# Two convs at a time: pairing the convolution steps of a fused dynamic-conv and feed-forward kernel

## The chip, the cores and the metric

The kernel runs on one core of one Trainium2 chip. The core has five engines with a queue each: TensorE (PE; its weight loads are shown as PEld), VectorE (DVE), ScalarE (ACT), GpSimd (POOL) and SyncE (SP). Each works through its own instructions in order and waits on semaphores for the others. The metric is the device time of one execution in microseconds; the median of three runs of the kernel before is 729.72 us (729.19 to 730.9).

## The reference

```
# x (8, 4096, 192), weight_gen (8, 4096, 8 heads, 7 taps), w_in (192, 2048), w_out (2048, 192)
w = softmax(weight_gen over the 7 taps)
x_pad = x with 6 zero rows ahead of each sequence
y[b, s, h, :] = sum over k of w[b, s, h, k] * x_pad[b, s + k, 24 columns of head h]
out = (max(y @ w_in, 0) ** 2) @ w_out        # y as 32768 rows of 192
```

Each token has its own seven weights for each of eight heads; the result goes through a feed-forward layer with squared ReLU.

## The kernel before

The 32768 tokens are cut into sub-blocks of 512 tokens. Blocks 0 and 1 have one sub-block, blocks 2 to 32 have two (`BLOCKS`), so block j, from 2 on, holds sub-blocks 2j - 2 and 2j - 1. Blocks are worked on in an interleaved order that the program writes out by hand (`tc.manual_schedule()`): each engine's instructions stand in the order in which the program issues them. There is one such order for each block, a string of steps (`plans[j]`), in which

- `u` is a unit (`st_unit`, line 571): six matmuls of 512 columns, with 64-row weights in two row halves, make 128 hidden features of the block's 1024 tokens in a two-bank PSUM tile `h`. ScalarE applies ReLU into `t1` (line 595), and VectorE squares two units at a time into `g` (line 599). 16 units make a block: u0 to u15 below.
- `M` is half a quarter of the second matrix product of the block before (`st_mm2`, line 611): 32 matmuls of 192 columns (line 630) that read 8 of the 16 chunks of `g`. Two M make a quarter: the first reads chunks 0 to 7, the second 8 to 15. They add up in the two PSUM banks `o0` and `o1`, of which there is one each. After the second M `o_sum` has ScalarE copy `o0` (line 644) and VectorE add `o1` (line 646), and only then can the next quarter's first M write there. M0 to M7 below; the sums follow M1, M3, M5 and M7, and after M3 and M7 SyncE stores the result (line 651).
- `C` is the conv of the next block (`st_conv_spread`, line 481, from block 8 on): 80 matmuls with 32-column weights taken from `x`, moving the band tiles `bd`. They fill two PSUM tiles `yp` of two banks, of which ScalarE copies the first to SBUF and VectorE the second (line 512). Then SyncE moves a few rows inside `y` (line 516, four DMAs).
- `B` is the band work of one sub-block (`st_bands`, line 658): VectorE multiplies the softmax rows `wr` with a mask into a band tile `bd` (line 406), in one instruction, or in two where a batch begins or ends. The conv needs both band tiles of its block.
- `L`, `E`, `S` are load, exponentials (ScalarE, line 244) and the rest of the softmax on VectorE (lines 251, 258, 266) of one piece of a batch's tokens. A batch from number 3 on has pieces of 8, 10, 10 and 10 rows for each partition. After its last piece the weights are stored to DRAM (line 280), and SyncE loads rows of them (`wr_load`, lines 317 to 327), which the bands read.

`h`, `yp` share three two-bank tiles of PSUM that go round (tag `h`), `o0` and `o1` are the other two banks. In the steady state a block's order is

```
steady_spread = "MuMuuu" * 2 + "MuCMuuu" + "MuMuuu"
```

that is M0 u0 M1 u1 u2 u3, M2 u4 M3 u5 u6 u7, M4 u8 C M5 u9 u10 u11, M6 u12 M7 u13 u14 u15. Steps B, E, S and L are put ahead of a unit by `at(j, u, kind, ...)`, line 769: the bands of block j + 1 ahead of units 1 and 5 of block j, the four softmax pieces of a batch whose first block is f ahead of unit 9 of blocks f - 5 to f - 2 (`TIMES`, line 775, gives other places to the early batches). `x_load` (line 329, on GpSimd's queue) follows the conv, and `load_rows` (line 826) asks at the start of block j for the rows of block j + 2.

Of the kernel before, what the change touches and what calls it, by code (L numbers as in the profile page):

```python
# [9 lines left out]
def kernel(  # L10
# [35 lines left out]
    G = D // H  # L46
    SPREAD = H - 2
    FIRST_SPREAD = 8
    HP = H // 2

    P = 128
# [344 lines left out]
    def st_band(j, tiles):  # L396


        if j not in bd_t:
            bd_t[j] = p_bd.tile([P, H * NT * STEP], f16, name="bd")  # L400
        i = tiles[0]
        lo = STEP * i
        shift = 0 if i == 0 and j % NBB == 0 else lo - tile_start(j, i)
        n = min(STEP, P - shift)
        shape = (P, HP * len(tiles), n // SL, 2 * SL)
        nc.vector.tensor_tensor(  # L406
            out=bd_t[j][:, H * lo : H * (lo + len(tiles) * n)].rearrange(
                "p (g m c) -> p g m c", g=shape[1], c=2 * SL
            ),
            in0=wr_t[j][:, i : tiles[-1] + 1]  # L410
            .rearrange("p t g c -> p (t g) c")
            .unsqueeze(2)
            .broadcast_to(shape),
            in1=mask[:, shift : shift + n]
            .rearrange("p (m c) e -> p m (c e)", c=SL)
            .unsqueeze(1)
            .broadcast_to(shape),
            op=AluOp.mult,
        )
# [58 lines left out]
        else:  # L478
            nc.scalar.copy(out=y[:, 0:2], in_=yp)

    def st_conv_spread(j):

        s0, n = BLOCKS[j]
        y = p_y.tile([P, NK + 1, TB], f16, name="y")
        y_t[j] = y
        for ks in ((NK, NK - 1), (0, 1)):
            yp = ps_h.tile([P, 2, TB], f32, name="yp", tag="h")
            k0 = min(ks)
            for k in ks:
                for i in range(NT):  # L490
                    a, b = bounds[i], bounds[i + 1]
                    for half in (0, 1):
                        s = s0 + half
                        hi = a + (STEP if tile_start(s, i) == starts[i] else b - a)
                        bd = bd_t[s][:, H * a : H * hi].rearrange(
                            "p (g c e) -> p g e c", g=HP, e=2
                        )
                        for e in (0, 1):
                            head = 2 * k + e
                            p0 = RT * half + 32 * e  # L500
                            c0 = min(G * head, D - 32)
                            nc.tensor.matmul(  # L502
                                out=yp[p0 : p0 + 32, k - k0, a:b],
                                lhsT=x_t[s][:, i, c0 : c0 + 32],
                                rhs=bd[:, head // 2, e, 0 : b - a],
                                start=True,
                                stop=True,
                                skip_group_check=True,
                                tile_position=(0, p0),
                            )  # L510
            copy = nc.vector.tensor_copy if k0 == 0 else nc.scalar.copy
            copy(out=y[:, k0 : k0 + 2], in_=yp)  # L512
        for p0 in range(0, P, 32):
            head = SPREAD + p0 // 32 % 2
            r0 = p0 + G * head - min(G * head, D - 32)
            nc.sync.dma_start(out=y[p0 + G : p0 + 32, 0:NK], in_=y[r0 : r0 + G, NK])

    def st_conv(j):

        if j >= FIRST_SPREAD:  # L520
            return st_conv_spread(j)
# [144 lines left out]
    with nc.allow_low_precision("fp16 matmul pipeline"), tc.manual_schedule():  # L666
# [80 lines left out]
        for q in range(4):  # L747
# [7 lines left out]

        steady = "MuMuuu" * 3 + "MuuuMCu"
        steady_spread = "MuMuuu" * 2 + "MuCMuuu" + "MuMuuu"
        plans = {
# [10 lines left out]
        def at(j, u, kind, *args):  # L769
# [26 lines left out]
        for n, s in enumerate(parts[4:], 4):  # L796
            b, f = s.b, s.fb
            k = n - min(m for m, p in enumerate(parts) if p.b == b)
            times = TIMES.get((b, k)) or (
                (f - 5, 9), (f - 4, 9), (f - 3, 9), (f - 2, 9)  # L800
            )
            assert len(times) == len(s.pieces)
            for j, u in times:
                at(*exp_time(j, u), "E", n)
                at(j, u, "S", n)
            at(times[0][0] - 1, 0, "L", n)
        for j in range(len(plans), NBLK - 1):
            a = BLOCKS[j + 1][0]
            small = [p for p in parts if p.fb <= j + 1][-1].r == FIRST
            us = {4: (7, 9), 6: (7, 9)}.get(j, (5, 9) if small else (1, 5))  # L810
            if j + 1 >= FIRST_SPREAD:
                us = (1, 5)
            for n, u in enumerate(us):
                at(j, u, "B", a + n)
        for j in range(len(plans), NBLK):
            plan, u = [], 0
            for step in steady_spread if j + 1 >= FIRST_SPREAD else steady:
# [56 lines left out]

        mm2 = quarters()
        for j in range(NBLK):
            if j + 2 < NBLK:
                load_rows(j + 2)
            if j == 1:
                for q in range(WQ):  # L880
                    cross_w_in(q)
            u = 0
            for step in plans[j].split():
                kind, n = step[0], int(step[1:] or 0)
                if kind == "u":
                    st_unit(j, u)
                    u += 1
                elif kind == "M":
                    next(mm2)
                elif kind == "C" and j + 1 < NBLK:  # L890
                    st_conv(j + 1)
                    if j == 0:
                        x_load(3)
                    elif j + 2 < NBLK:
                        for k in range(BLOCKS[j + 2][0], sum(BLOCKS[j + 2])):
                            x_load(k)
                    if j == 5:
                        load_w_spread()
                    elif j == 6:
                        cross_w_spread()  # L900
                elif kind == "E":
                    parts[n].exp(*next(parts[n].exps))
                elif kind == "S":
                    soft(parts[n])
                elif kind == "B":
                    st_bands(n)
                elif kind == "L":
                    parts[n].load(nc.sync)
# [47 lines left out]
```

## Time and profile before

The profiled execution has a span of 728.43 us (first to last instruction); the runs, timed around the whole execution, have a median of 729.72 us. The granted TensorE clock is 1.000.

| engine | busy us | share of the span | instructions |
|---|---|---|---|
| PE | 722.0 | 99% | 14078 |
| PEld | 530.1 | 73% | 14078 |
| DVE | 625.8 | 86% | 839 |
| ACT | 612.0 | 84% | 731 |
| POOL | 98.5 | 14% | 146 |

| work | line | engine | count | busy us | mean ns of one |
|---|---|---|---|---|---|
| second product (M) | 630 | PE | 8032 | 380.1 | 243 |
| units, from block 8 on | 581 | PE | 2400 | 291.7 | 376 |
| convs, from block 8 on | 502 | PE | 2000 | 28.4 | 210 |
| ReLU | 595 | ACT | 512 | 496.6 | 1027 |
| square | 599 | DVE | 287 | 307.4 | 1105 |
| bands | 406 | DVE | 90 | 149.5 | 1685 |
| add of o1 | 646 | DVE | 123 | 68.4 | 556 |

How to read it: matmuls are pipelined, so the mean of one is a latency and not its share of the time; what a step costs is read from the distance between starts. [...]

### The profile page before, as it was taken

The page shows a single profiled execution, that of the slowest core. Times are in us where ns is not written, and L with a number is a line of the kernel's source. Part 1 is how long each engine was busy: PE and PEld are TensorE (multiplying, and loading weights), DVE is VectorE, ACT ScalarE, POOL GpSimd, SP SyncE. Part 2 cuts the span into 40 slices and gives each one's busy share as a digit, 9 for nine tenths or more (in the row PEclk, how much of TensorE's full clock was granted, in tenths as well). Part 3 has the DMA queues.
Part 4 walks back from the last instruction along what each step waited for, and adds up shares of the span by engine and source line. Part 5 has one row for each costly group of instructions (what it writes and reads, how often), then busy time and mean ns, then how long its engine had stood idle before and what let it go on. Part 6 is the DMA issues. An engine that isn't in the chain of part 4 may idle for free.

```text
span 728.4 us, 31046 instructions
## 1 busy us (share of the span) xinstructions
PE 722.0 (99%) x14078; PEld 530.1 (73%) x14078; DVE 625.8 (86%) x839; ACT 612.0 (84%) x731; POOL 98.5 (14%) x146
## 2 busy tenths in 40 slices
PE   8999999999999999999999999999999999999998
PEld 5668877777777777777777777777777777777777
DVE  7999997998898998888988888988888988778753
ACT  6998888888888888888888888888888888888883
POOL 7231223411001100011001010010000110001000
PEclk9999999999999999999999999999999999999999
DMA  9664465676245443356432554343544325444112
GB/s 193 128 113 106 82 125 89 128 142 138 78 71 133 99 84 68 75 116 125 83 62 58 135 104 88 66 74 110 114 78 87 57 53 117 67 87 77 30 46 67
DMA packets 126272, 68.30 MB, mean 94 GB/s; under 512 B 85353, under 2 KB 122556, under 8 KB 125628
## 3 DMA queue, kind: packets, MB, share of 16 engines
q0 software_dynamic: 46192, 19.43, 22.9%
q1 hardware_dynamic: 79804, 46.79, 22.5%
q8 instruction: 110, 1.80, 1.1%
q14 instruction: 22, 0.18, 0.1%
q10 hardware_dynamic: 144, 0.10, 0.0%
HBM read 50.18 MB, written 28.70 MB: 108 GB/s over the span
## 4 chain that ended last, share of the span: by engine, by line
PE 98%; DMA 1%; SPq 0%; ACT 0%; issue 0%; ACTq 0%
PE o L630 47%; PE h L581 44%; PE yp L502 4%; PE h L566 2%; PE yp L536 1%; DMA w_st<-in_moe_w_in_dram 1%; SPq L219 0%; PE yp L466 0%; ACT w_i L740 0%; SPq L135 0%; SPq L133 0%; ACT y L476 0%; SPq L327 0%; SPq L317 0%; ACT o_sb L644 0%
## 5 line engine op out<-in xcount | busy, mean ns | idle before, releaser
L595 ACT ACTIVATE t<-h 128x1024 f16<-128x1024 f32 x512 | 496.6, 1027 | 60.1 <-PE h L581 58.4
L630 PEld LDWEIGHTS <-g 64*128 64x128 f16 (+1 forms) x8032 | 344.3, 94 | 55.2 <-issue 2.3
L630 PE MATMUL o<-w_o,g 64*128 64x192 f16 (+1 forms) x8032 | 380.1, 243 | 0.1
L599 DVE TENSOR_TENSOR g<-t 128x2048 f16<-128x2048 f16 (+1 forms) x287 | 307.4, 1105 | 28.7 <-ACT t L595 28.3
L581 PE MATMUL h<-y,w_p 64*128 64x512 f16 x2400 | 291.7, 376 | 0.0
L581 PEld LDWEIGHTS <-w_p 64*128 64x128 f16 x2400 | 113.9, 94 | 94.8
L406 DVE TENSOR_TENSOR bd<-wr,mask 128x4160 f16<-128x4160 f16 (+4 forms) x90 | 149.5, 1685 | 1.2 <-ACT wr L391 1.2
L646 DVE TENSOR_TENSOR o_sb<-o,o_sb 128x384 f32<-128x384 f32 x123 | 68.4, 556 | 61.4 <-ACT o_sb L644 60.3
L327 POOL DMA_DIRECT2D xt<-in_x_dram x63 | 52.6, 838 | 415.4 <-PE yp L502 362.5
L644 ACT COPY o_sb<-o 128x384 f32<-128x384 f32 x129 | 61.6, 477 | 45.7 <-PE o L630 44.4
L581 PE MATMUL h<-y,w_i 64*128 64x512 f16 x576 | 70.5, 376 | 0.0
L581 PEld LDWEIGHTS <-w_i 64*128 64x128 f16 x576 | 30.5, 94 | 21.7 <-issue 1.2
L502 PEld LDWEIGHTS <-xt 128*32 128x32 f16 x2000 | 24.6, 95 | 10.6 <-issue 10.6
L266 DVE TENSOR_TENSOR v_big<-ex,rcp 128x112 f16<-128x112 f32 (+5 forms) x180 | 29.9, 237 | 2.1 <-DMA vd<-v_big 1.1
L512 DVE CAST y<-yp 128x1024 f16<-128x1024 f32 x25 | 30.4, 1218 | 0.0
L502 PE MATMUL yp<-bd,xt 128*32 128x104 f16 (+1 forms) x2000 | 28.4, 210 | 0.0
L244 ACT ACTIVATE ex<-wg 128x560 f32<-128x560 f32 (+5 forms) x40 | 26.3, 659 | 1.2 <-DMA wg<-in_weight_gen_dram 1.2
L251 DVE TENSOR_REDUCE ssum<-ex 128x80 f32<-128x560 f32 (+5 forms) x40 | 25.6, 639 | 1.3 <-ACT ex L244 1.3
L512 ACT CAST y<-yp 128x1024 f16<-128x1024 f32 x25 | 25.2, 1007 | 0.0
L258 DVE RECIPROCAL rcp<-ssum 128x64 f32<-128x64 f32 (+4 forms) x39 | 23.0, 589 | 1.4
L317 POOL DMA_DIRECT2D xt<-in_x_dram x7 | 3.9, 555 | 120.4 <-PE yp L502 109.4
L361 POOL DMA_DIRECT2D wr<-v_first x24 | 13.0, 559 | 24.0 <-DVE v_first L266 23.8
(42 smaller groups left out, 111.9 us busy)
## 6 DMA issues: line engine op xcount, KB each, us to landing
out_dram<-o_sb SPq DMA_DIRECT2D x63, 384.0 KB
xt<-in_x_dram POOLq DMA_DIRECT2D x42, 240.0 KB, 4.9
wg<-in_weight_gen_dram SPq DMA_DIRECT2D x4, 1064.0 KB
xt<-in_x_dram POOLq DMA_DIRECT2D x21, 192.0 KB, 5.0
wr<-vd SPq DMA_DIRECT2D x38, 80.0 KB
vd<-v_big SPq DMA_DIRECT2D x5, 512.0 KB
y<-y SPq DMA_DIRECT2D x100, 24.0 KB
wg<-in_weight_gen_dram SPq DMA_DIRECT2D x3, 616.0 KB
```

The costliest lines, as they stand in the source:

```text
L244: nc.scalar.activation(out=self.ex[:, lo:hi].rearrange("p r g k e -> p (r g) k e"), in_=self.wg[:, lo:hi].rearrange("p r (g e) k -> p (r g ...
L266: eng.tensor_tensor(out=bass.AP(tensor=v.tensor, offset=v.offset + lo * H * SL + lo % SL * 2 + g * SL * 2, ap=[list(v.ap[0]), [H * SL + 2, ...
L327: eng.dma_start(out=dst[:, first:last], in_=ap)
L406: nc.vector.tensor_tensor(out=bd_t[j][:, H * lo : H * (lo + len(tiles) * n)].rearrange("p (g m c) -> p g m c", g=shape[1], c=2 * SL), in0= ...
L502: nc.tensor.matmul(out=yp[p0 : p0 + 32, k - k0, a:b], lhsT=x_t[s][:, i, c0 : c0 + 32], rhs=bd[:, head // 2, e, 0 : b - a], start=True, sto ...
L512: copy(out=y[:, k0 : k0 + 2], in_=yp)
L581: nc.tensor.matmul(out=h[:, half], lhsT=w_in_chunk(w, u, slot, half), rhs=y_t[j][r0 : r0 + RT, k], start=(slot == 0), stop=(slot == NK - 1 ...
L595: nc.scalar.activation(out=t1[:, e], in_=h, func=ActF.Relu)
L599: nc.vector.tensor_tensor(out=g[:, a : e + 1], in0=t1[:, a : e + 1], in1=t1[:, a : e + 1], op=AluOp.mult)
L630: nc.tensor.matmul(out=oo[:, cc * Dm : (cc + 1) * Dm], lhsT=g[r0 : r0 + n, cc * P : (cc + 1) * P], rhs=w_o[r0 : r0 + n, fc, :], start=(fc ...
L644: nc.scalar.copy(out=o_sb, in_=o[0][:, c])
L646: nc.vector.tensor_tensor(out=o_sb, in0=o[1][:, c], in1=o_sb, op=AluOp.add)
```

## The change

From block 14 on every second block (14, 16 ... 30) has a step `D` in place of `C`: it runs the convs of the next two blocks, one right after the other, and the blocks between have no conv. In the order of such a block, D stands behind M5, where C stood ahead of it:

```
steady_pair = "MuMuuu" * 2 + "MuMDuuu" + "MuMuuu"
```

Four PSUM tiles are filled by a pair. Three are `yp` tiles of the ring; the fourth, the last of the second conv, is put into `o0` and `o1`, one bank each, and VectorE copies it in two instructions of 512 columns. Around this:

- bands: those of block j + 2 (not j + 1) are made in block j, ahead of units 1 and 5; of block 15 ahead of unit 13 of block 13 and unit 0 of block 14, of block 16 ahead of units 2 and 6 of block 14. Every fourth band tile from block 15 on is put into the memory of `w_i`, the weights of the units before block 8.
- rows: from block 12 on, those of block j + 3 are asked for (block 12 asks for 14 and 15).
- softmax: the pieces of a batch come one block sooner, in blocks f - 6 to f - 3; for batch 4 (f = 17) ahead of units 1 and 9 of block 12 and unit 9 of blocks 13 and 14.
- x: loaded for two blocks after each D, and for blocks 15 and 16 after the conv in block 13.
- buffers: `p_x` four (before two), `p_wr` six (four), `p_y` three (two).

```diff
-    p_x = ctx.enter_context(tc.tile_pool(name="p_x", bufs=2))
-    p_wr = ctx.enter_context(tc.tile_pool(name="p_wr", bufs=4))
+    p_x = ctx.enter_context(tc.tile_pool(name="p_x", bufs=4))
+    p_wr = ctx.enter_context(tc.tile_pool(name="p_wr", bufs=6))
...
-    p_y = ctx.enter_context(tc.tile_pool(name="p_y", bufs=2))
+    p_y = ctx.enter_context(tc.tile_pool(name="p_y", bufs=3))
...
+        first = BLOCKS[FIRST_PAIR + 1][0]
+        if j not in bd_t and j >= first and (j - first) % 4 == 3:
+            bd_t[j] = w_i.rearrange("p q e c -> p (q e c)")[:, 0 : H * NT * STEP]
...
+    def st_conv_spread(blocks):
+
+        for j in blocks:
+            y = p_y.tile([P, NK + 1, TB], f16, name="y")
+            y_t[j] = y
+            for ks in ((NK, NK - 1), (0, 1)):
+                k0 = min(ks)
+                copy = nc.vector.tensor_copy if k0 == 0 else nc.scalar.copy
+                if j != blocks[0] and k0 == 0:
+                    outs = [ps_o.tile([P, TB], f32, name=f"yo{k}", tag=f"o{k}") for k in ks]
+                    spread_slots(j, ks, outs)
+                    for k, o in zip(ks, outs):
+                        copy(out=y[:, k], in_=o)
+                else:
+                    yp = ps_h.tile([P, 2, TB], f32, name="yp", tag="h")
+                    spread_slots(j, ks, [yp[:, k - k0] for k in ks])
+                    copy(out=y[:, k0 : k0 + 2], in_=yp)
+            spread_rows(y)
...
         steady_spread = "MuMuuu" * 2 + "MuCMuuu" + "MuMuuu"
+        steady_pair = "MuMuuu" * 2 + "MuMDuuu" + "MuMuuu"
+        steady_plain = "MuMuuu" * 4
...
+            (4, 0): ((12, 1), (12, 9), (13, 9), (14, 9)),
...
-                (f - 5, 9), (f - 4, 9), (f - 3, 9), (f - 2, 9)
+                (f - 6, 9), (f - 5, 9), (f - 4, 9), (f - 3, 9)
...
+        a = BLOCKS[FIRST_PAIR + 1][0]
+        at(FIRST_PAIR - 1, 13, "B", a)
+        at(FIRST_PAIR, 0, "B", a + 1)
+        for j in range(FIRST_PAIR, NBLK - 2):
+            a = BLOCKS[j + 2][0]
+            for n, u in enumerate((2, 6) if j == FIRST_PAIR else (1, 5)):
+                at(j, u, "B", a + n)
...
-            if j + 2 < NBLK:
+            if j + 2 < NBLK and j <= FIRST_PAIR - 2:
                 load_rows(j + 2)
+            if j + 3 < NBLK and j >= FIRST_PAIR - 2:
+                load_rows(j + 3)
...
+                elif kind == "D":
+                    if j + 2 < NBLK:
+                        st_conv_spread([j + 1, j + 2])
+                    if j + 4 < NBLK:
+                        for k in range(BLOCKS[j + 3][0], sum(BLOCKS[j + 4])):
+                            x_load(k)
```

`FIRST_PAIR` is 14. `spread_slots(j, ks, outs)` holds the conv's loop of matmuls as it was, for the slots `ks` into the given PSUM tiles, and `spread_rows(y)` the four moves of rows.

More of the change, by code (lines that the diff above doesn't have):

```diff
@@ L48 @@
     FIRST_SPREAD = 8
+    FIRST_PAIR = 14
     HP = H // 2
@@ L479, in st_conv_first @@
             nc.scalar.copy(out=y[:, 0:2], in_=yp)
[L481 to L496, printed above, removed]
-                        )
[L498 to L512, printed above, removed]
@@ new lines, in spread_slots @@
+    def spread_slots(j, ks, outs):
+        s0 = BLOCKS[j][0]
+        for k, out in zip(ks, outs):
+            for i in range(NT):
+                a, b = bounds[i], bounds[i + 1]
+                for half in (0, 1):
+                    s = s0 + half
+                    hi = a + (STEP if tile_start(s, i) == starts[i] else b - a)
+                    bd = bd_t[s][:, H * a : H * hi].rearrange(
+                        "p (g c e) -> p g e c", g=HP, e=2
+                    )
+                    for e in (0, 1):
+                        head = 2 * k + e
+                        p0 = RT * half + 32 * e
+                        c0 = min(G * head, D - 32)
+                        nc.tensor.matmul(
+                            out=out[p0 : p0 + 32, a:b],
+                            lhsT=x_t[s][:, i, c0 : c0 + 32],
+                            rhs=bd[:, head // 2, e, 0 : b - a],
+                            start=True,
+                            stop=True,
+                            skip_group_check=True,
+                            tile_position=(0, p0),
+                        )
@@ L513, in st_conv_spread, with spread_rows @@
+    def spread_rows(y):
         for p0 in range(0, P, 32):
@@ L516, in st_conv_spread @@
             nc.sync.dma_start(out=y[p0 + G : p0 + 32, 0:NK], in_=y[r0 : r0 + G, NK])
+    def st_conv_spread(blocks):
[15 more added lines that the diff above has]
+            spread_rows(y)
     def st_conv(j):
         if j >= FIRST_SPREAD:
-            return st_conv_spread(j)
+            return st_conv_spread([j])
         if j < NFIRST:
@@ L812 @@
                 us = (1, 5)
+            if j >= FIRST_PAIR:
+                break
             for n, u in enumerate(us):
+                at(j, u, "B", a + n)
[5 more added lines that the diff above has]
+            for n, u in enumerate((2, 6) if j == FIRST_PAIR else (1, 5)):
                 at(j, u, "B", a + n)
@@ L816 @@
             plan, u = [], 0
-            for step in steady_spread if j + 1 >= FIRST_SPREAD else steady:
+            form = steady_spread if j + 1 >= FIRST_SPREAD else steady
+            if j >= FIRST_PAIR:
+                form = steady_plain if (j - FIRST_PAIR) % 2 else steady_pair
+            for step in form:
                 if step == "u":
@@ L894 @@
                     elif j + 2 < NBLK:
-                        for k in range(BLOCKS[j + 2][0], sum(BLOCKS[j + 2])):
+                        last = j + 3 if j + 1 == FIRST_PAIR else j + 2
+                        for k in range(BLOCKS[j + 2][0], sum(BLOCKS[last])):
                             x_load(k)
```

## The prediction

> **What bounds the kernel now.** I read first the chain of work that ended last, then the groups by line, then the timelines of TensorE, VectorE and ScalarE block by block, and last SyncE's queue. The chain, by engine:
>
> ```profile
> PE 98%; DMA 1%; SPq 0%; ACT 0%; issue 0%; ACTq 0%
> ```
>
> From 97 us on TensorE's steps repeat to within 0.03 us and none waits for another engine. So time is won only by taking TensorE's steps away, and a wait put in front of TensorE is lost for good. Two groups by line (count | busy us, mean ns of one | idle before):
>
> ```profile
> L512 DVE CAST y<-yp 128x1024 f16<-128x1024 f32 x25 | 30.4, 1218 | 0.0
> ...
> L477 DVE CAST y<-yp 128x512 f16<-128x512 f32 x1 | 0.7, 692 | 0.5 <-PE yp L466 0.5
> ```
>
> One block in the timeline (start us, duration); its first M starts at 406.34, the next block's at 428.41, 22.07 later. TensorE about its conv, then VectorE:
>
> ```profile
> 412.89 0.81 PE L581 MATMUL h<-y,w_p 64*128 64x512 f16 x6
> 413.53 1.49 PE L630 MATMUL o<-w_o,g 64*128 64x192 f16 x32
> 414.85 2.11 PE L581 MATMUL h<-y,w_p 64*128 64x512 f16 x18
> 416.80 1.48 PE L630 MATMUL o<-w_o,g 64*128 64x192 f16 x32
> 418.12 0.81 PE L581 MATMUL h<-y,w_p 64*128 64x512 f16 x6
> 418.86 1.11 PE L502 MATMUL yp<-bd,xt 128*32 128x104 f16 x80
> 419.90 1.49 PE L630 MATMUL o<-w_o,g 64*128 64x192 f16 x32
> ```
>
> ```profile
> 410.33 0.56 DVE L646 TENSOR_TENSOR o_sb<-o,o_sb 128x384 f32<-128x384 f32 x1 [1.50 <-ACT o_sb L644]
> 410.81 2.31 DVE L406 TENSOR_TENSOR bd<-wr,mask 128x4160 f16<-128x4160 f16 x1
> 413.04 2.35 DVE L599 TENSOR_TENSOR g<-t 128x2048 f16<-128x2048 f16 x2
> 415.56 0.56 DVE L646 TENSOR_TENSOR o_sb<-o,o_sb 128x384 f32<-128x384 f32 x1 [0.17 <-ACT o_sb L644]
> 416.04 2.35 DVE L406 TENSOR_TENSOR bd<-wr,mask 128x3328 f16<-128x3328 f16 x2
> 418.30 2.35 DVE L599 TENSOR_TENSOR g<-t 128x2048 f16<-128x2048 f16 x2
> 420.57 1.22 DVE L512 CAST y<-yp 128x1024 f16<-128x1024 f32 x1
> 421.94 0.56 DVE L646 TENSOR_TENSOR o_sb<-o,o_sb 128x384 f32<-128x384 f32 x1
> 422.42 0.73 DVE L251 TENSOR_REDUCE ssum<-ex 128x80 f32<-128x560 f32 x1
> 423.18 0.65 DVE L258 RECIPROCAL rcp<-ssum 128x80 f32<-128x80 f32 x1
> 423.87 1.22 DVE L266 TENSOR_TENSOR v_big<-ex,rcp 128x56 f16<-128x56 f32 x8
> 425.00 2.35 DVE L599 TENSOR_TENSOR g<-t 128x2048 f16<-128x2048 f16 x2
> 427.28 0.55 DVE L646 TENSOR_TENSOR o_sb<-o,o_sb 128x384 f32<-128x384 f32 x1
> ```
>
> Read here: a unit ahead of an M takes 0.64 us (412.89 to 413.53), the same unit ahead of a conv 0.74 (418.12 to 418.86). And VectorE's add of line 646 must come before the next quarter's M: that of 415.56 ends 0.7 us ahead of the M at 416.80. VectorE's long idle time, 1.50 us, lies before M1's add, not after it.
>
> **Removed: two switches for each pair.** In the single matmul records the last unit matmul to the first conv matmul is 0.306 us, to the first M matmul 0.212; the last conv matmul to the first M matmul is 0.137, where four conv matmuls take 0.049 inside a conv (0.929 / 19). So each change between the 64-row and the 32-column form costs about 0.09. A pair of convs back to back has two changes and not four. By transitions: before, two blocks hold 2 x (0.306 + 0.137) and 14 unit-to-M, 16 M-to-unit; after, one M-to-conv (0.172, from the four of the older conv, line 536), one conv-to-unit (0.136), one join (0.049), 16 x 0.212, 15 x 0.079 (M-to-unit). The difference is 0.886 - 0.357 - 0.424 + 0.079 = 0.18. With nine pairs (in blocks 14, 16 ... 30): 1.7 us won. Bounds: 0.17 to 0.23 for a pair, 1.5 to 2.1.
>
> [...]
>
> **Put in place of it: waits of the pair.** Block clock, zero at its first M; M0..M7 and u0..u15 as they come. M5 starts at 12.42 (unit u8 at 11.78 plus 0.65), the pair at 12.42 + 1.24 + 0.17 = 13.83, its second conv at 14.77, its last matmul at 15.70, u9 at 15.84, M6 at 17.78, M7 at 19.75, the next block at 23.01. A matmul that waits for VectorE or ScalarE starts 0.05 after that one's end (11.06 to 11.12 us). ScalarE's copy of an o starts 1.52 after its M, the add of line 646 0.51 later and takes 0.56; a conv tile can be read some 0.23 after its last matmul's start.
> - Fourth tile of the pair, in o0 and o1, from 15.24: M5's add starts at 14.45 (VectorE's g ends at 14.23, as above) and ends at 15.01. Room 0.2.
> - u9 needs the first tile, which ScalarE copies 14.55 to 15.56; room 0.2. u10 (16.49) needs the second, VectorE 14.99 to 16.21; room 0.2. u11 (17.14) needs the third, ScalarE to 16.5.
> - M6 (17.78) needs o1 back. The copy of 1024 columns (1.218) becomes two of 512 (0.692 each by line 477): starts at 16.13 and 16.74, end 17.43. Room 0.3. (At most, if each half took 1.218, o1 would come 0.7 late, 6 us over nine; the row of its own shape decides.)
> - Then a softmax piece of ten rows (422.42 to 425.00: 2.59), two g (1.14 each from start to start) and M7's add, 22.21 to 22.77; the next M0 at 23.01. Room 0.2.
> So nothing waits in these pairs, narrowly; cover gone, each 0.1 us costs up to 0.9 over nine. Bounds: 0 and 0.2 a pair, 1.8 in all; I take 0.
>
> The split copy costs VectorE 2 x 0.692 - 1.218 = 0.166 a pair, 1.5 over nine, inside the 0.3 of room ahead of M6. [...]
>
> **Moved: softmax pieces, and here it costs.** Batch 4's first piece goes to block 12, unit 1. In VectorE's order it stands behind M1's add, ahead of the first band. That add starts at 3.99 (410.33 - 406.34), then: 0.48 to the next, eight rows 1.99 (356.15 to 358.14 in the trace), the band 2.27 (in two pieces, 416.04 to 418.30), two g 2.27. M3's add starts at 11.00, ends at 11.55, and M4, due at 10.46, goes on at 11.60. **Lost: 1.1 us.** Without the piece the add was ready at 9.22. Bounds 0.9 to 1.3 by these rows' spread. Later in that block I find no wait: M5's add ends 0.25 before M6.
>
> **Moved: four bands around the start of block 14.** Beyond block 13's own two they stand at (13, unit 13), (14, 0), (14, 2) and (14, 6). In block 13, after M7's add at 20.94: band 21.41 to 23.64 (2.23), g of u12 and u13 to 24.78, the two single g of 0.61 and 0.68 to 26.07. Block 14's M1 (22.07 + 1.97 = 24.04) reads that last g as its eighth chunk at 25.13; it goes on at 26.2. **Lost 1.05.** The band of (14, 0) then runs 26.0 to 28.23, M1's add 28.23 to 28.79, and M2, now due at 28.4, starts at 28.84. **Lost 0.45.** After that, M4 has 0.25 of room, and the pair finds M5's add done 0.3 ahead of need. Bounds: 0 if a band could hide in idle time (there are 1.5 us of it in a block, all before M1's add, and 2.23 + 2.23 don't fit), 2.2 if M2 waits the whole second band; I take 1.5 by the row sum.
>
> **Other moves, costed at nothing.**
> - SyncE: a pair issues eight y moves (0.72 each, 5.75 together) ahead of the softmax store, not four: from 16.3 to 22.0. The store of batch b goes out at 22.1, not 18.8. It takes 3.4 to land (425.12 to 428.48), the row loads, the second issued 0.4 after the first, 1.6 and 2.1 (landed 430.07 and 430.96): at 27.1 and 27.9. The bands that read them come at 27.47 and 28.0, where 2.4 us were to spare. Past that, VectorE has 0.2 before M3's add and M4 0.6 after it. If the landing is 1.8 later, 1 us is lost in each of the four blocks 14, 18, 22, 26.
> - x on GpSimd, with four buffers: its wait for the conv (362.5 us on line 327) becomes shorter, and the loads (4.9 us to land) have a block or more before use. Rows of the block three ahead: six buffers, more lead. The fourth band in w_i, which nothing reads after block 7: same instruction. ScalarE's exponentials move a block; its conv copies stay 1.0 us each, two in a row after M5, counted above.
>
> **Sum.** -1.7 + 1.1 + 1.05 + 0.45 = +0.9 us on a profiled span of 728.43: 729.3. The median of the runs is 729.72, 1.3 above that span (start and end around it); I keep this 1.3: **730.6 us**.
>
> **Rivals.**
> 1. *Faster: the waits of blocks 12 to 14 are not there.* For it: VectorE sits idle 1.5 us before M1's add, and 86% busy is an average. Against: the order is fixed, and the idle time lies ahead of that add. With no such wait 729.72 - 1.7 = 728.0. 13%.
> 2. *Slower: VectorE's queue behind each pair.* One mechanism, in each of blocks 14 to 30: after the pair come three copies in a row and, up to block 26, the softmax piece and two g ahead of M7's add. It decides once VectorE is 0.2 us later than in my sum. For it: four rooms of 0.2 to 0.3 in a row. Against: the row of line 477, and that VectorE reaches 14.23 in all blocks I compared. If it is 0.5 late, 0.3 x 9 = 2.7 on top: 733.3. 25%.
> 3. *The pair saves nothing:* the change of form is hidden by the reorder of weight loads (their engine idles 10.6 us before line 502, 0.42 each). Against: 0.306 and 0.212 are starts of matmuls, on the engine that bounds. It would give 729.72 + 2.6 = 732.3. 4%.
>
> **How the numbers follow.** My forecast has 58%; its own range is 729.6 to 732.0 (saving 1.5 to 2.1, blocks 12 to 14 2.0 to 3.2, pairs 0 to 0.6). Runs can't tell changes under 0.2% (1.46 us) apart: 728.26 to 731.18 counts as the same. The forecast puts 0.46 in it and 0.12 above. Rival 2 (0.25) and 3 (0.04) add to slower: 0.41. Rival 1 has its 0.13 about the limit at 728.26; I give 0.12 to faster, 0.01 to the same, which has 0.47. The range 728.2 to 733.2 leaves out half of rivals 1 and 2.
>
> **What would show it.** In the changed profile: nine runs of 160 conv matmuls, 0.17 after an M and 0.14 before a unit; in block 12 an M4 (some 10.5 us after the block's M0) that starts about 1.1 late behind VectorE's line of the add; in block 14 an M1 that stretches from 1.24 to some 2.3 us, and an M2 0.45 late; elsewhere no M or unit waiting. The forecast is wrong if TensorE waits in every pair for o1 or a conv copy, if bands wait for rows from DRAM in blocks 15, 19, 23, 27, or if M4 of block 12 is on time.

## The result: slower by 1.5%

| kernel | median of the runs, us | runs | span of the profiled execution, us | granted clock |
|---|---|---|---|---|
| before | 729.82 (729.19 to 730.9) | 4 | 728.4 | 1.000 |
| changed | 740.7 (740.05 to 741.25) | 4 | 739.4 | 1.000 |

The ratio is 1.0148, with a 95% interval of 1.0134 to 1.0163. The forecast was 730.6, with a range up to 733.2: the change costs some 11 us where 0.9 was expected.

### The profile page after: what moved, and what is told of

Same layout as the page of the kernel before. It is cut to its first block, busy times and chain, and to the rows that moved or that the text cites. A ratio compares the mean times of both kernels' runs of the same rounds, so it can differ in the third digit from the quotient of the medians.

```text
span 739.4 us, 31005 instructions
## 1 busy us (share of the span) xinstructions
PE 723.9 (98%) x14078; PEld 553.5 (75%) x14078; DVE 627.4 (85%) x848; ACT 613.6 (83%) x731; POOL 98.3 (13%) x146
## 4 chain that ended last, share of the span: by engine, by line
PE 51%; DVE 3%; DMA 3%; issue 1%; SPq 0%; ACT 0%
PE o L649 26%; PE h L600 23%; PE yp L501 2%; DMA vd<-v_big 1%; DVE g L618 1%; DMA y<-y 1%; DVE bd L410 1%; DMA wr<-vd 1%; PE yo L501 0%; DVE v_big L267 0%; DVE y L534 0%; DVE y L530 0%; SPq L516 0%; DVE o_sb L665 0%; DVE rcp L259 0%
## 5 line engine op out<-in xcount | busy, mean ns | idle before, releaser
L649 PEld LDWEIGHTS <-g 64*128 64x128 f16 (+1 forms) x8032 | 363.9, 94 | 51.7 <-issue 8.2
L649 PE MATMUL o<-w_o,g 64*128 64x192 f16 (+1 forms) x8032 | 397.3, 243 | 4.7 <-DVE o_sb L665 4.2
L600 PE MATMUL h<-y,w_p 64*128 64x512 f16 x2400 | 308.3, 376 | 2.2 <-issue 1.9
L600 PEld LDWEIGHTS <-w_p 64*128 64x128 f16 x2400 | 135.0, 94 | 90.5 <-issue 2.7
L410 DVE TENSOR_TENSOR bd<-wr,mask 128x4160 f16<-128x4160 f16 (+4 forms) x76 | 128.9, 1715 | 6.9 <-DMA wr<-vd 6.1
L501 PE MATMUL yp<-bd,xt 128*32 128x104 f16 (+1 forms) x1460 | 22.5, 209 | 0.0
L410 DVE TENSOR_TENSOR w_i<-wr,mask 128x3328 f16<-128x3328 f16 (+2 forms) x14 | 21.0, 1531 | 0.0
```

The source lines that it names most:

```text
L410: nc.vector.tensor_tensor(out=bd_t[j][:, H * lo : H * (lo + len(tiles) * n)].rearrange("p (g m c) -> p g m c", g=shape[1], c=2 * SL), in0= ...
L501: nc.tensor.matmul(out=out[p0 : p0 + 32, a:b], lhsT=x_t[s][:, i, c0 : c0 + 32], rhs=bd[:, head // 2, e, 0 : b - a], start=True, stop=True, ...
L600: nc.tensor.matmul(out=h[:, half], lhsT=w_in_chunk(w, u, slot, half), rhs=y_t[j][r0 : r0 + RT, k], start=(slot == 0), stop=(slot == NK - 1 ...
L649: nc.tensor.matmul(out=oo[:, cc * Dm : (cc + 1) * Dm], lhsT=g[r0 : r0 + n, cc * P : (cc + 1) * P], rhs=w_o[r0 : r0 + n, fc, :], start=(fc ...
```

## The profile after

The chain of work that ended last, by engine, in the changed kernel. It reaches back only to 302.5 us, so its shares add up to some 59% of the span and can't be set beside the 98% for TensorE before, where the chain goes back to the start:

```profile
PE 51%; DVE 3%; DMA 3%; issue 1%; SPq 0%; ACT 0%
```

TensorE is still busy for 723.9 us (722.0 before), so it was given no more work. It waits. Its waits in the changed kernel (line, what was waited for: us in total, times, longest):

```profile
PE o L649 <- DVE o_sb L665: 4.2, 5, 1.5
PE yo L501 <- issue: 2.3, 3, 1.1
PE h L600 <- issue: 1.9, 2, 1.1
```

None of the three rows is there before. "issue" means that nothing in the profile ended the wait. To place each wait, I compared the distance from every unit's first matmul to the next one's in the two traces, from block 2 to block 32. The differences add up to 11.3 us (the first of these units is 0.35 earlier, which leaves the 10.9 between the spans):

| where | us | what ends the wait |
|---|---|---|
| nine pairs, by themselves | -2.0 | a block with an unhindered pair is 0.95 longer, the one after it 1.15 to 1.20 shorter |
| block 12, M4 and the conv behind it | +1.3 | the add of line 665 |
| block 14, M1 and M2 | +1.45 | the last g (0.93), the add (0.52) |
| block 6, the M that starts at 134.01 | +1.7 | the add, behind a band that waited for its rows |
| in or behind the pairs of blocks 14, 16, 22, 24, 30 | +5.25 | "issue": 0.7, 1.1, 1.3, 1.3, 0.9 |
| M4 of blocks 19 and 27 | +1.9 | the add, behind bands that waited for rows |
| first unit of blocks 19 and 21 | +0.7 | the y moves |
| M5 ahead of the pairs of blocks 18, 22, 26, 30 | +0.8 | not found: 1.62 us to the pair's first matmul, 1.41 to 1.52 in the other five |
| all else | +0.15 | differences under 0.08 each |

The first three rows are the forecast's own terms (-1.7, +1.1, +1.5). In TensorE's timeline of the changed kernel (start us, duration) the waits of blocks 12 and 14 look like this; an M that waits is split into its first matmul and the rest:

```profile
263.49 0.24 PE L649 MATMUL o<-w_o,g 64*128 64x192 f16 x1
264.66 1.48 PE L649 MATMUL o<-w_o,g 64*128 64x192 f16 x31 [0.93 <-DVE o_sb L665]
...
300.48 1.82 PE L649 MATMUL o<-w_o,g 64*128 64x192 f16 x28
302.56 0.34 PE L649 MATMUL o<-w_o,g 64*128 64x192 f16 x4 [0.26 <-DVE g L618]
...
304.68 0.24 PE L649 MATMUL o<-w_o,g 64*128 64x192 f16 x1
305.26 1.48 PE L649 MATMUL o<-w_o,g 64*128 64x192 f16 x31 [0.34 <-DVE o_sb L665]
```

M1 of block 14 does not stop in one place: its first 28 matmuls stretch over 1.82 us, where all 32 take 1.48 elsewhere.

The other rows, some 10 us, are missing from the forecast's sum. All but the last two of them have three sources.

**Block 6.** VectorE's timeline, changed and then before:

```profile
131.78 2.33 DVE L410 TENSOR_TENSOR bd<-wr,mask 128x4160 f16<-128x4160 f16 x1 [1.81 <-DMA wr<-vd]
```

```profile
130.25 2.32 DVE L406 TENSOR_TENSOR bd<-wr,mask 128x4160 f16<-128x4160 f16 x1
```

The same band starts 1.5 us later because its rows do, though they were asked for 3.6 us sooner (121.93 and not 125.52 on SyncE's queue). What is new beside them is GpSimd's copy of `w_p` (weights of the units), two transfers of 384 KB:

```profile
121.79 1.31 POOL L171 DMA_DIRECT2D w_p<-w_p  x2
```

With two x buffers GpSimd's next x loads waited for a conv (at 95 and 118 us before) and held everything behind them on its queue. With four they don't: the loads of `w_p` begin at 104.3 and not at 120.2, and this copy comes at 121.8 and not at 144.7, while SyncE reads the rows. TensorE's M then waits for the add behind the band:

```profile
135.76 1.48 PE L649 MATMUL o<-w_o,g 64*128 64x192 f16 x31 [1.51 <-DVE o_sb L665]
```

The copy is named by its time alone: the x loads asked for just ahead of it (119.58 to 121.82, and 142.48 before) came sooner too, and no run tells the two apart.

**Rows and y moves from block 14 on.** SyncE's queue at the pair of block 18, changed and then a block with the same store before: y moves, the softmax store, the first row load, which waits for the store to land:

```profile
406.30 5.72 SPq L516 DMA_DIRECT2D y<-y  x8
412.13 0.39 SPq L281 DMA_DIRECT2D vd<-v_big  x1
417.60 0.34 SPq L318 DMA_DIRECT2D wr<-vd  x1
```

```profile
421.86 2.83 SPq L516 DMA_DIRECT2D y<-y  x4
425.12 0.34 SPq L280 DMA_DIRECT2D vd<-v_big  x1
428.50 0.35 SPq L317 DMA_DIRECT2D wr<-vd  x1
```

From store to row load it takes 5.5 us and not 3.4. The DMA queue with the x loads (packets, MB, share of 16 engines) from 405 to 420 us, and the same from 418 to 432 us before, shows twice the traffic:

```profile
q0 software_dynamic: 2640, 0.98, 58.2%
```

```profile
q0 software_dynamic: 1328, 0.49, 31.8%
```

The x loads of two blocks start as soon as the pair has read the old ones (405.23), beside the store. The bands that read the late rows then hold up the add, and the add M4 of block 19:

```profile
419.27 0.59 DVE L410 TENSOR_TENSOR bd<-wr,mask 128x832 f16<-128x832 f16 x1 [1.27 <-DMA wr<-vd]
420.09 1.89 DVE L410 TENSOR_TENSOR bd<-wr,mask 128x3328 f16<-128x3328 f16 x1 [0.23 <-DMA wr<-vd]
...
424.17 0.55 DVE L665 TENSOR_TENSOR o_sb<-o,o_sb 128x384 f32<-128x384 f32 x1
...
424.77 1.42 PE L649 MATMUL o<-w_o,g 64*128 64x192 f16 x30 [0.63 <-DVE o_sb L665]
```

**Waits that nothing ends.** TensorE at the pair of block 16 in the changed kernel:

```profile
358.65 1.18 PE L501 MATMUL yp<-bd,xt 128*32 128x104 f16 x82
...
360.67 0.82 PE L600 MATMUL h<-y,w_p 64*128 64x512 f16 x5
362.29 1.68 PE L600 MATMUL h<-y,w_p 64*128 64x512 f16 x13 [0.80 <-issue]
```

The pair itself runs through, 320 instructions (160 weight loads, 160 matmuls) in 1.87 us. Then unit 9 stops after five of its six matmuls, in the middle of a group whose data is there. The profile's list of DMA queues has one whose kind is named for what could be missing:

```profile
q8 instruction: 110, 1.80, 1.0%
```

110 packets of 16384 bytes. Over TensorE's 28156 loads and matmuls that is 64.0 bytes for each, so 256 to a packet. That the queue is TensorE's is an estimate from this agreement; no view says it. Set beside the five waits (times from the trace's packets and matmuls):

```
pair in block   packet from, to   TensorE stops, goes on   goes on after the packet's end
14              313.70  314.64    315.43  316.13           1.49
16              359.68  360.93    361.11  362.29           1.36
22              494.00  494.93    495.12  496.39           1.46
24              539.96  540.89    540.82  542.32           1.43
30              673.22  674.54    674.94  675.85           1.31
```

And counted in program order from the first one of the trace (TensorE's few semaphore instructions included), all five stops are at instruction 194 or 195 of a group of 256, a weight load and its matmul. By the same count the pairs begin at instruction 182, 190 and 198 of their group (blocks 14, 22, 30), 120 and 128 (16, 24), 58 and 66 (18, 26), 252 and 4 (20, 28); only the first two kinds stop.

## The experiments

Each expectation names its own theories; a letter does not stand for the same one in all of them. Of the edits the main lines are shown: e1 is set against the kernel before, e2 to e7 against the changed kernel, e9 and e8 against e7, e10 against e8, e11 against e10. "Before" was run again beside each set: 730.22 (e1 to e4), 729.55 (e5 to e8), 729.74 us (e9 to e11).

**e1_px4: the kernel before, with four x buffers alone.**

```diff
-    p_x = ctx.enter_context(tc.tile_pool(name="p_x", bufs=2))
+    p_x = ctx.enter_context(tc.tile_pool(name="p_x", bufs=4))
```

> The kernel before with four x buffers in place of two, nothing else. In the profile of the changed kernel block 6, long before the first pair, has a wait of 1.7 us: VectorE stood 1.81 us ahead of a band until rows that SyncE had asked for at 121.93 us landed at 131.76, while GpSimd's 768 KB of w_p to w_p copies ran from 121.8 to 131.6. In the kernel before, GpSimd sent these copies later, because its x loads waited for a conv. Theory A (the buffers let GpSimd run ahead, and its copies collide with the row loads): about 731.5, +1.7 us over before, with the wait in block 6. Rival B (the wait comes from another part of the change, such as p_wr or p_y): as before, 729.8, and no wait in block 6.

731.22 us, ratio 1.0014 (1.0004 to 1.0024). In its trace block 6 is 2.24 longer, by a wait of the same M, nothing else moves by more than 0.2 and the start is 0.64 shorter. The buffers alone make the wait of block 6.

**e2_shift: 128 more TensorE instructions ahead of everything.** The warm-up's matmuls are narrower and more.

```diff
-        WARM = 156
+        WARM = 64
...
-        spin(46)
+        spin(110)
```

> The changed kernel with 110 warm-up matmuls of 64 columns in place of 46 of 156: 128 TensorE instructions more (a load and a matmul each) ahead of everything, so that all later ones stand 128 further along the 256-instruction (16 KB) pieces in which the queue of instruction loads brings them; nothing else moves. In the changed kernel five TensorE waits that no engine ends (0.7 to 1.3 us, after the pairs of blocks 14, 16, 22, 24, 30; 5.2 us in all) stop at places 194 or 195 of 256. Theory A (the pair uses up instructions faster than they are loaded): the waits leave 14, 16, 22, 24, 30 and appear in blocks 18, 20, 26, 28; four of them, total 739 to 741. Rival B (contention with the x loads or another transfer after the pair): the same five blocks wait, 740.7.

741.25 us, 1.0148 (1.0115 to 1.0182). The waits without a releaser left blocks 14, 16, 22, 24 and 30 and came up in 18, 20, 26 and 28 (matmul gaps of 0.82, 1.52, 0.60, 1.95 us):

```profile
PE yo L501 <- issue: 2.8, 3, 1.7
PE h L600 <- issue: 1.1, 1, 1.1
```

These are exactly the pairs that now begin where the stopping ones did, at 186 and 194 (blocks 18, 26) and 124 and 132 (20, 28), and they stop at instruction 194 or 195 again. Only the place in the stream was changed for these pairs, and the waits went with it, as theory A has it. The total stayed, because where a pair no longer stopped, rows or y moves were late (0.37 to 1.3 us in blocks 17, 19, 23, 25).

**e3_half: a conv of half as many instructions.** From block 15 on one matmul of 64 weight columns stands for the two of 32; the second head of each pair of heads is not computed.

```diff
+                    w = 64 if j > FIRST_PAIR else 32
-                    for e in (0, 1):
+                    for e in (0,) if w == 64 else (0, 1):
...
-                            out=out[p0 : p0 + 32, a:b],
-                            lhsT=x_t[s][:, i, c0 : c0 + 32],
+                            out=out[p0 : p0 + w, a:b],
+                            lhsT=x_t[s][:, i, c0 : c0 + w],
```

> The changed kernel whose convs from block 15 on have one matmul with 64 weight columns where there were two with 32 (the second head of a pair of heads gets the first one's band, so its part of the conv is not computed). The moving columns and so the time of a conv stay, but a pair issues 160 TensorE instructions, not 320. Theory A (instruction supply): no wait without a releasing engine after any pair; 5.2 us less, 735 to 736. Rival B (contention after the pair): the five waits stay, 740 to 741.

No pair is followed by a wait without a releaser: the theory of the instruction supply holds again. The time is 740.25 (1.0102 to 1.0176), a miss: M4 of blocks 23 and 27, on time or 1.0 late in the changed kernel, is 2.1 and 2.3 late here, of blocks 15 and 19 0.7. TensorE came sooner to bands whose rows came no sooner.

**e4_xlate: the x loads moved in the program.** They follow unit 9 of the next block in the order in which the program issues them.

```diff
-        steady_plain = "MuMuuu" * 4
+        steady_plain = "MuMuuu" * 2 + "MuMuXuu" + "MuMuuu"
...
-                    if j + 4 < NBLK:
-                        for k in range(BLOCKS[j + 3][0], sum(BLOCKS[j + 4])):
+                elif kind == "X":
+                    if j + 3 < NBLK:
+                        for k in range(BLOCKS[j + 2][0], sum(BLOCKS[j + 3])):
                             x_load(k)
```

> The changed kernel with the x loads of a pair sent a block later (behind unit 9 of the odd block, still 20 us ahead of use) and not right after the pair. In the changed kernel the softmax store after the pairs of blocks 18 and 26 took 5.4 and 5.1 us to land where 3.4 were measured before, so that bands and with them M4 of blocks 19 and 27 came 0.95 late, and u0 of blocks 19 and 21 waited 0.3 and 0.4 for y rows. Theory A (the four x loads crowd out the store and the y moves): these waits vanish, 2.5 us less, 738; the waits without a releaser stay, since they are not contention. Rival B (the eight y moves ahead of the store on SyncE's queue are all of it): they stay, 740.7. Rival C (the x loads also hold up the instruction loads): the five waits without a releaser vanish too, 733.

741.03 us. But the edit did nothing: GpSimd has nothing else to do there and asks for x when the buffers come free, at 315.69 us as at 315.27, wherever the program writes it. So this tells no theory apart. It is a second execution of the same schedule, and shows how much rows vary: M4 of block 19 was 0.2 late (0.94 in the changed kernel), of 27 1.7 (0.97), of 15 0.6 (0).

**e5_xgate: x held back for good.** A copy of one column on GpSimd, which needs g of unit 9 of the odd block, stands ahead of the x loads at step X.

```diff
+                elif kind == "X":
+                    if j + 3 < NBLK:
+                        nc.gpsimd.tensor_copy(out=gate, in_=g_t[(j, 9)][:, 0, 0:1])
+                        for k in range(BLOCKS[j + 2][0], sum(BLOCKS[j + 3])):
+                            x_load(k)
```

> The x loads of a pair held back on GpSimd until g of unit 9 of the odd block is there (a one-column copy of that g into gate stands ahead of them), so that they no longer run beside the pair's row moves and the softmax store. Theory D (two blocks of x, 0.98 MB, fill the DMA engines while the 512 KB softmax store, the row loads and the y moves want them): the store lands in 3.5 to 4 us and not in 5.1 to 5.5, the waits of M4 in blocks 15, 19, 23, 27 and of u0 go, about 2.6 to 3 us, and the waits that no engine ends stay: 737.7 to 738.2. Rival Q (the store goes out 2.9 us late because eight y moves stand ahead of it on SyncE): 740.7, nothing moves. Rival C (the x traffic is also what makes the instruction pieces late): the five waits without an engine shrink as well, down to about 733.

SyncE's store and first row load of block 18 here:

```profile
414.45 0.38 SPq L281 DMA_DIRECT2D vd<-v_big  x1
417.19 0.34 SPq L318 DMA_DIRECT2D wr<-vd  x1
```

2.7 us, though eight y moves still stand ahead of the store; and no M4 and no first unit from block 15 on waits. D holds, Q falls, and C too: the waits without a releaser in 14, 16, 24 and 30 are 1.1, 1.0, 1.2 and 0.5 (0.7, 1.1, 1.3 and 0.9 in the changed kernel), clearly smaller in one block alone. The time, 740.97 us, is a miss for another reason. One pair now waits for x:

```profile
PE yp L501 <- DMA xt<-in_x_dram: 2.7, 1, 2.7
```

It is that of block 22: its x, asked for at 479.15, ran beside the 896 KB of softmax input that SyncE reads from 480.08 on, and its last packet ended at 497.55, 0.35 ahead of the conv's going on. The hold was too long. Two long waits were also followed by a lower clock (last section).

**e6_rowlate: the store ahead of the second four y moves.** These are asked for after unit 10.

```diff
-            spread_rows(y)
+            if j == blocks[0]:
+                spread_rows(y)
...
+                elif kind == "R":
+                    if j + 2 < NBLK:
+                        spread_rows(y_t[j + 2])
```

> The four y moves of the pair's second block asked for after unit 10 and not straight behind the pair, so that the softmax store stands behind four moves as before. Rival Q: the store is asked for 2.9 us sooner, the waits of M4 in 19 and 27 go and those of u0 stay: 738.6 to 738.9. Theory D: the store goes out into the same x traffic and lands about 1 us sooner: 739.5 to 740.2. Instruction supply: the five waits stay as they are.

740.29 us (1.0134 to 1.016), level with the changed kernel. The store of block 18 goes out sooner, in the full x traffic (0.63 MB from 410 to 418 us), and its rows can be read no sooner:

```profile
410.39 0.34 SPq L281 DMA_DIRECT2D vd<-v_big  x1
417.49 0.35 SPq L318 DMA_DIRECT2D wr<-vd  x1
```

7.1 us in place of 5.5, and M4 of blocks 19 and 27 is still 0.8 and 0.7 late. So not SyncE's queue but the traffic decides; D's own figure (1 us sooner) was too kind.

**e7_mended: four repairs.** e5 and e6 together, the x buffers as two pools of two (blocks up to 15 use only the first), and batch 4's first piece one unit sooner.

```diff
-            (4, 0): ((12, 1), (12, 9), (13, 9), (14, 9)),
+            (4, 0): ((12, 0), (12, 9), (13, 9), (14, 9)),
...
-    p_x = ctx.enter_context(tc.tile_pool(name="p_x", bufs=4))
+    p_x = ctx.enter_context(tc.tile_pool(name="p_x", bufs=2))
+    p_x2 = ctx.enter_context(tc.tile_pool(name="p_x2", bufs=2))
```

> Four repairs together: x held back, the second block's y moves late, the four x buffers as two pools of two of which only one serves the blocks ahead of 15, and the first softmax piece of block 12 at unit 0. If the account is complete: 740.7 less 1.7 (block 6), less 1.3 (block 12), less 2.6 to 3 (rows and y) = 734.7 to 735.1; what is left over 729.8 is 5.2 of waits without an engine and 1.45 in block 14, less 1.8 saved in the pairs. If rows stay late: 737 or more.

737.29 us (735.08 to 740.82; ratio 1.0109, 1.009 to 1.0129): short of the expected 734.7. Blocks 6 and 12 are level with the kernel before (0.0 each), no rows or y moves are late, but block 22 stands 3.09 us for its x, as in e5. Three of the six runs also had a lower granted clock (0.995 to 0.998), as all four of e5 had; they are the three slowest.

**e9_xsooner: the same, x held to unit 5 only.**

```diff
-        steady_plain = "MuMuuu" * 2 + "MuMuXuu" + "MuMuuu"
+        steady_plain = "MuMuuu" + "MuMuXuu" + "MuMuuu" * 2
...
-                        nc.gpsimd.tensor_copy(out=gate, in_=g_t[(j, 9)][:, 0, 0:1])
+                        nc.gpsimd.tensor_copy(out=gate, in_=g_t[(j, 5)][:, 0, 0:1])
```

> As the repaired kernel, with x released by g of unit 5 of the odd block and not of unit 9. There the pair of block 22 stood 3.09 us with its x as the releaser, where the changed kernel had 1.27 without a releaser, and a wait of that length was followed by a lower granted clock in some runs. If x was held too long: the wait in block 22 is 1.3 again, no clock below 1.0, 735.0 to 735.5 with a narrow spread, 5.2 to 5.6 over the kernel before, all but 1.45 of it behind waits that no engine ends. Rival (x is late because it always is, when two blocks are asked for at once): 737 again.

734.75 us (734.26 to 735.87; ratio 1.0065, 1.0052 to 1.0077), just under the 735.0 to 735.5 given. 5.0 us over the kernel before are left: 5.45 in waits without a releaser (blocks 14, 16, 22, 24, 30: 1.5, 0.8, 0.8, 1.5, 0.9), 1.45 in block 14, 0.5 in block 6, 0.35 in M5 of blocks 18 and 26, less 2.0 in the pairs, 0.25 in block 4 and 0.5 at the start. The account closes.

**e8_four: the repaired kernel, with pairs only where they don't stop.**

```diff
+        PAIRS = (18, 20, 26, 28)
...
-                form = steady_plain if (j - FIRST_PAIR) % 2 else steady_pair
+                form = steady_pair if j in PAIRS else steady_plain if j - 1 in PAIRS else steady_spread
```

> As the repaired one, with pairs only in blocks 18, 20, 26 and 28 (where the changed kernel showed no wait without an engine) and single convs in the others; x of a single conv's block is asked for behind its conv. Theory A (instruction supply stops a pair by where it stands in the stream): no such wait is left, 729.8 + 1.45 (block 14) - 4 x 0.2 = 730.4, within 0.5. Rival (a pair costs about 0.6 wherever it stands, and waits only hide it): 732 or more.

730.47 us, ratio 1.0013 (1.0004 to 1.0022), where 730.4 was expected; over the kernel before beside it that is 0.9 and not 0.65. No wait without a releaser is left, the rival (732 or more) falls, and M5 ahead of the pairs takes 1.41 us again. All that is left of TensorE's waits for VectorE is block 14:

```profile
PE o L652 <- DVE o_sb L668: 0.3, 1, 0.3
PE o L652 <- DVE g L621: 0.3, 1, 0.3
```

**e10_four_b and e11_none: another way into the new order, with four pairs and with none.** The bands come forward as one third band at unit 13 of blocks 14 and 15; x as in e9.

```diff
-        at(FIRST_PAIR - 1, 13, "B", a)
-        at(FIRST_PAIR, 0, "B", a + 1)
+        for n in range(3):
+            at(FIRST_PAIR, (1, 5, 13)[n], "B", a + n)
+            at(FIRST_PAIR + 1, (1, 5, 13)[n], "B", a + 3 + n)
...
-        PAIRS = (18, 20, 26, 28)
+        PAIRS = ()
```

> As the one with four pairs, with the bands drawn forward as a third band at unit 13 of blocks 14 and 15 in place of four in blocks 13 and 14. If the two waits of block 14 (0.94 and 0.51) came of bands too close together, they go: before less 4 x 0.2 = 0.8, 728.8. If a third band costs about 0.5 to 0.9 wherever it stands: 729.8 to 730.5.

> The same without any pair: single convs throughout, bands and rows a block sooner, x as in the kernel before. It shows what the four pairs save by themselves. If a pair that nothing stops saves 0.2: 0.8 above the one with four pairs, and level with the kernel before (729.6) if the third bands cost nothing. If a pair saves nothing: level with the one with four pairs.

731.27 us (1.0008 to 1.0026) and 731.39 us (1.0013 to 1.0031). Both expectations for e10 were too low. Each third band cost M1 of the next block 0.94 and 0.84 us, so this way in is no cheaper (1.8 against 1.45). By the blocks' lengths in the two traces the four pairs save 0.21, 0.20, 0.25 and 0.19, together 0.85. The medians don't show it: they differ by 0.12, where 0.8 was expected, with overlapping intervals. The spans of the two profiled executions differ by 1.4, more than the pairs, since in block 6 of e11 VectorE stood 1.86 us for a store of softmax rows to land (1.13 in the kernel before), which cost TensorE 0.66. What the pairs save is thus read from traces, not from times, and no version here beats the kernel before.

## Why the prediction was wrong, point by point

The terms that the forecast added up came out. It failed in the step "Other moves, costed at nothing", where two of the moves cost 4.3 us, and it had no term at all for the waits that nothing in the profile ends, which cost 5.25.

- *Two switches less for each pair, 0.18 for the pair (bounds 0.17 to 0.23).* Right: 0.20 to 0.25, nine times. The starts of the records, 0.306 and 0.212, gave it rightly. Rival 3 falls.
- *Block 12, 1.1 us.* Right: 1.10, and 0.23 behind it, where the forecast found no wait. Moving the piece by one unit took both away (e7).
- *Block 14, 1.05 and 0.45.* Right: 0.93 and 0.52. Rival 1 falls.
- *The pair's rooms of 0.2 to 0.3.* They held: no pair waits for o1 or for a conv copy, but for 0.13 us in block 14 of e2 and e3, where a unit waits for VectorE's copy. The two half copies (0.68 us each, 0.14 more than one of 1.22) cost TensorE nothing. Rival 2 falls: behind the pairs VectorE is late only where its rows are.
- *"SyncE ... It takes 3.4 to land."* Wrong: 5.1 to 5.5 in blocks 18, 22 and 26 (3.8 in 14). The figure came from a block in which one block's x was read, though the change asks for two there. The sentence after it priced the miss well (1.8 later, 1 us a block: 0.94 and 0.97 at 2.0 later), but in a side remark at no cost, and the only lateness that it reckoned with was that of the eight y moves. e5 and e6 name the traffic. It cost 1.9 us in two of the four blocks, and 0.7 for y moves. Bands that wait for rows were one of the forecast's own signs of being wrong, and blocks 19 and 27 show it.
- *"x on GpSimd, with four buffers: its wait for the conv becomes shorter."* The failed step behind block 6, 1.7 us: I asked only whether x would be late. Such waits, at 95 and 118 us (15.6 and 15.5 us, for the older conv of line 536, not among the 362.5), also held back the loads and the copy of `w_p` queued behind them; let go, these met the row loads of batch 2 (e1).
- *The term that is missing:* the waits that nothing ends, 5.25 us, nearly half of the loss; e2 and e3 bear out the theory that TensorE's own instructions come too late there. A pair issues 320 in 1.87 us, where they go at 28156 in 739.4 us, 71 in 1.87 us, on the average. The profile of before gave no warning of it: the idle time that it puts down to "issue" ahead of the conv's weight loads (rival 3) is the same 0.42 us ahead of each of the 25 convs, wherever it lies in the stream.

What isn't settled: the 0.2 us of M5 ahead of four pairs; why the stops fall on instruction 194 or 195 (no view shows where in the program a packet begins); what sets the length of a stop, which varies from 0.5 to 2.1 us between executions; and whether a single conv is free of stops only because it is short (no run here has one that stops).

## What to carry to other kernels

- Ask of a denser stretch not only whether its data is there but whether its instructions are: count what an engine issues in it (here 320 in 1.87 us against 71 on the average), and look for a queue whose bytes agree with that count (64.0 for each). Where a wait has no releaser, shift the stream and see if the wait moves with it (e2: from blocks 14, 16, 22, 24 and 30 to 18, 20, 26 and 28).
- GpSimd's waits for a conv, 15.6 and 15.5 us, were also a gate for all that stood behind them: without them the loads of `w_p` began at 104.3 us and not at 120.2. Before a buffer is added, list what that queue does next, and whose transfers this will meet. Moving a line in the program moved nothing on an engine that only waited for buffers (e4: 315.69 us as at 315.27); it took a dependence (e5), and a hold to unit 9 was too long (2.7 us of wait for x), one to unit 5 was not (e9: none).
- Merging two steps doubled what they trigger at one moment: 0.98 MB of x and not 0.49, beside which a store took 5.5 us to its row load and not 3.4. A landing time is to be read under that load, not in the step alone.

## What the runs showed of the hardware

- The queue that the profile calls "instruction" moved 110 packets of 16384 bytes in the changed kernel, about 1 us each (0.88 to 1.7); by the estimate of 64.0 bytes for each TensorE load and matmul, a packet holds 256. After each of the five waits that nothing ends, TensorE went on 1.3 to 1.5 us after the end of such a packet (up to 1.6 in e2). A stretch of 320 instructions in 1.87 us met such a wait in five of nine places, one of 160 in 0.93 us (the single convs) in none. In seven executions (the changed kernel, e2, e4, e5, e6, e7, e9) all 32 such stops are at instruction 194 or 195 of 256.
- In e5's profiled execution two waits of TensorE (2.20 us from one matmul's start to the next in block 6, 2.91 in block 22) were followed by stretches at a lower granted clock. Windows of that execution (us, busy time of PE, PEld, DVE, ACT and POOL, then the granted clock, DMA share, GB/s), behind the wait in block 22 and behind the one in block 6:

```profile
497.90:499.40 1.50, 1.50 (x82) 1.14 (x84) 0.55 (x1) 0.79 (x1) 0.00 (x0) 0.85 0.24 66
499.40:502.80 3.40, 3.40 (x24) 1.33 (x22) 3.33 (x13) 2.28 (x4) 0.00 (x0) 0.56 0.10 27
502.80:507.00 4.20, 4.20 (x82) 3.23 (x78) 2.69 (x3) 2.79 (x4) 0.00 (x0) 1.00 0.39 144
...
137.00:140.60 3.60, 3.60 (x29) 2.49 (x26) 3.53 (x3) 1.20 (x2) 0.00 (x0) 0.53 0.02 5
140.60:144.00 3.40, 3.40 (x160) 3.02 (x158) 2.52 (x4) 2.65 (x4) 0.00 (x0) 1.00 0.00 0
```

What is missing to a clock of 1.00 in these windows adds up to 1.7 us for each stretch, an estimate of what it cost. A wait of 3.09 us in e7's profiled execution had no such stretch after it; the windows of the wait and behind it:

```profile
489.50:492.70 3.20, 0.31 (x26) 0.16 (x15) 1.54 (x2) 0.87 (x1) 0.00 (x0) 1.00 0.10 25
492.70:496.00 3.30, 3.30 (x104) 2.15 (x106) 2.35 (x4) 2.40 (x3) 0.00 (x0) 1.00 0.14 37
```

So a wait of 2.20 us was followed by a lower clock once and one of 3.09 us was not. Two executions show this and none tests it; what decides it is not shown.
